# Block-sorted attention and a spatial-gated MLP on one core: a new written order, masks by head pairs, and last output tiles in two goes

## The chip, the core and the metric

The kernel runs on one core of a Trainium2 chip. The core has a matrix engine (TensorE, "PE" in the profile, with its weight loads as "PEld"), a vector engine (VectorE, "DVE"), an engine for activation functions (ScalarE, "ACT"), a general engine (GpSimd, "POOL") and a queue engine (SyncE, "SP"). Sixteen DMA engines move data between the large memory and the core. Matrix products land in PSUM, a memory of eight banks, and another engine has to copy them out. The metric is the device time of one execution in microseconds (us), as the median of several runs. Lower is better.

## What is computed

```python
# q, k, v: 4 batches x 8 heads x 768 positions x 64; sort_net: 4 x 8 x 8 x 8
P = sort_net
for _ in range(5):
    P = np.exp(P - np.max(P, axis=-1, keepdims=True))
    P = P / (np.sum(P, axis=-1, keepdims=True) + 1e-09)
    P = P / (np.sum(P, axis=-2, keepdims=True) + 1e-09)
k_sorted = np.einsum('bhij,bhjcd->bhicd', P, k_b)   # blocks of 96 positions
v_sorted = np.einsum('bhij,bhjcd->bhicd', P, v_b)
attn = softmax(scale * q_b @ k_sorted^T)            # within each block
x = (attn @ v_sorted), heads side by side           # 4 x 768 x 512

h = np.maximum(x @ w_in, 0.0)                       # 512 -> 1024
u, v = h[..., :512], h[..., 512:]
v_n = (v - mean(v)) / np.sqrt(var(v) + 1e-06)
v_s = np.einsum('ts,bsd->btd', w_spatial, v_n) + b_spatial[None, :, None]
out = (u * v_s) @ w_out                             # 4 x 768 x 512
```

## The kernel before

The program is written as small units of work, the functions `u_XX`. One long text, `ORDER` (lines 16 to 49), lists the units in sequence, each with its arguments separated by colons; the loop at the end of the kernel runs through it. Every engine takes its instructions in that order and never overtakes within its own queue. So the order written there sets what stands behind what on each engine, and each DMA queue (loads are issued by POOL, all other transfers by SP) too.

The first argument of a unit that uses TensorE is the PSUM bank at which its tile starts; most tiles take two banks, and the next unit on those banks waits until the last one has been copied out. A letter A, D or P says which engine copies a result out (or does the unit's elementwise part): ACT, DVE or POOL. The following numbers are mostly batch, head pair (of four), and half of the blocks.

- `L` and `LH` load q, k, v (768 KB per batch, cast on the way), the two halves of w_in (`wv`, `wu`), w_spatial (`ws`) and w_out (`wo`), all on POOL's queue (lines 156 to 212). Tiles of q, k and v have two buffers each.
- `SK` is one round of the normalisation of P (lines 243 to 256). `PR` spreads P over partitions with eight small matmuls. `P0` multiplies it by a mask on DVE and so makes the mixing matrix of batch 0 (line 269); `PC` copies it out and `PD` makes the matrices of the other batches on POOL (line 281). `DM` are matmuls on zeros, with no result that is used (line 290).
- `QT` turns q of a head pair (line 324). `KT` mixes and turns k (line 339). For batch 0, `VT` mixes and turns v by the same matmul line, and `VX` turns it back into 96-row blocks (`vb`, line 378). For later batches, `VM` mixes v (`vm`, line 390) and `VC` gathers the blocks by eight DMAs per batch on SP (line 405). `QX` copies q together on DVE or POOL (lines 179 and 181) and turns it by a transposing DMA on SP (line 183), for the third and fourth batches.
- `SC` makes the scores of a head pair and half (line 423) and ACT takes their exponential (line 436). `AT` multiplies by v (line 448). DVE then takes a reciprocal (459) and divides (460). In the form with P, ACT first copies the product out to a scratch tile (`xr`, line 456), and POOL divides. The scratch tile has the tag "z" with two buffers, the same two that `SP` uses for its sums.
- `XT` turns x for batch 0 on TensorE (line 472); `XX` does it by a transposing DMA on SP (line 190) for the others. `WT` is a tiny POOL copy that lets the next load on POOL's queue wait for such a transfer.
- `VP` (line 491) and `UP` (line 536) are the two halves of x @ w_in. `VP` also takes mean and variance on DVE. `LN` and `LA` normalise v, `LA` on DVE or POOL.
- `WS` turns w_spatial by TensorE (line 297). `SP` is the spatial product of 128 columns (line 548), with the bias added on DVE (`z`, line 554) and the product with u (`gt`, line 560) on DVE or POOL. `SH` is half of such a unit (lines 568 to 577).
- `OP` makes two tiles of the output (line 597) and sends them out on SP (line 605). `OH`, used for the last six tiles, makes one (line 583), into one of three buffers (line 587).

In the order before, loads are issued as q (first heads), k, v, q (other heads), `wv`, `wu`, `ws`, then v and k of the second batch, q of the second batch, `wo`, and then the third batch. The fourth batch's loads stand behind a `WT`.

## Time and profile before

| | us |
|---|---|
| median of five runs | 159.28 |
| lowest and highest run | 158.91, 161.5 |
| the profiled execution | 162.13 |
| its span in the trace | 160.2 |

| engine | busy us in the span |
|---|---|
| PE | 143.3 |
| DVE | 117.6 |
| ACT | 83.6 |
| POOL | 53.9 |

| line and work of PE | matmuls | busy us |
|---|---|---|
| 548, spatial product | 180 | 31.2 |
| 536, u half of x @ w_in | 128 | 23.0 |
| 491, v half of x @ w_in | 90 | 22.7 |
| 597, output | 67 | 16.4 |
| 448, attention times v | 256 | 12.7 |

The durations of matmuls overlap, as they are pipelined: twelve of line 548, 0.326 us each, take 1.95 us in the chain of waits. A row's busy time is thus more than it costs the engine, and spacing is read from the chain or the timeline. A few matmul records are missing in a trace. The chain of waits follows the span back from its last instruction, each time to what released it. Its pieces are listed with start, length and what they are. "Issue" in it is time for which the profile shows no cause. The mean granted clock of PE is 0.973 of full speed over the span.

### The profile page before, as it was taken

What the parts mean: (1) busy time and instruction counts of PE and PEld (TensorE: products, weight loads), DVE (VectorE), ACT (ScalarE), POOL (GpSimd) and SP (SyncE); (2) the same over time, 40 slices, a digit from 0 to 9 for tenths busy, and PEclk for the clock granted to TensorE, in tenths of its full rate; (3) what the DMA queues carried; (4) which work ended last, traced back from release to release, by engine and by line L of the source; (5) the groups of instructions that cost most, each with busy time, mean ns of one, the idle gap of its engine ahead of it and who ended that gap; (6) DMA issues with size and microseconds to landing.
All of it is one profiled execution on the core that took longest, in us unless ns stands there. A gap on an engine that the chain in (4) does not pass through costs nothing.

```text
span 160.2 us, 3907 instructions
## 1 busy us (share of the span) xinstructions
PE 143.3 (89%) x1605; PEld 90.5 (56%) x1617; DVE 117.6 (73%) x231; ACT 83.6 (52%) x127; POOL 53.9 (34%) x78
## 2 busy tenths in 40 slices
PE   0399979999998999999799988999999999999780
PEld 0396869755866665565466644655566545555330
DVE  3767867569798589679765999785768878649830
ACT  3325978559969445766754143788743225410140
POOL 7963910474700251060560380061400502500400
PEclk9999996599999999999999999999999999999997
DMA  2999999999999969979999989660745503042073
GB/s 15 198 204 204 207 211 206 203 205 206 226 250 248 192 109 90 227 108 176 220 286 244 194 141 183 109 118 0 262 135 98 97 5 131 0 174 87 0 262 133
DMA packets 36689, 25.49 MB, mean 159 GB/s; under 512 B 16576, under 2 KB 33472, under 8 KB 36672
## 3 DMA queue, kind: packets, MB, share of 16 engines
q0 software_dynamic: 14864, 12.19, 48.9%
q1 hardware_dynamic: 21808, 13.06, 35.6%
q8 instruction: 12, 0.20, 0.5%
q14 instruction: 5, 0.04, 0.1%
HBM read 24.78 MB, written 6.29 MB: 194 GB/s over the span
## 4 chain that ended last, share of the span: by engine, by line
PE 58%; DMA 17%; DVE 12%; issue 5%; SPq 3%; POOL 1%; ACT 1%; DVEq 0%; ACTq 0%; POOLq 0%
PE ps L548 14%; PE ps L536 10%; PE ps L491 10%; DMA vb<-vm 10%; PE ps L597 7%; DMA v_in<-in_v_dram 6%; PE ps L448 4%; PE ps L423 4%; DVE z L554 4%; PE ps L339 3%; SPq L405 3%; DVE gt L560 2%; DVE x_sb L460 1%; DMA out_dram<-oh_sb 1%; DVE stats L505 1%
## 5 line engine op out<-in xcount | busy, mean ns | idle before, releaser
L548 PE MATMUL ps<-wspT,v_sb 128*128 128x384 bf16 x180 | 31.2, 326 | 0.0
L436 ACT ACTIVATE ex<-ps 96x768 bf16<-96x768 f32 x32 | 24.5, 807 | 10.8 <-PE ps L423 10.8
L536 PE MATMUL ps<-xT,w_in_sb 128*128 128x384 bf16 x128 | 23.0, 326 | 0.9 <-DMA xT<-x_sb 0.6
L491 PE MATMUL ps<-w_in_sb,xT 128*128 128x512 bf16 x90 | 22.7, 386 | 0.9 <-DVE z L554 0.4
L548 PEld LDWEIGHTS <-v_sb 128*128 128x128 bf16 x180 | 17.0, 98 | 10.9
L460 POOL TENSOR_TENSOR x_sb<-xr,rec 96x512 bf16<-96x512 f32 x8 | 8.3, 1038 | 40.1 <-DVE rec L459 40.1
L554 DVE TENSOR_TENSOR z<-ps,b_bc 128x768 f32<-128x768 f32 x15 | 14.3, 953 | 5.4 <-PE ps L548 5.3
L505 DVE BATCH_NORM_STATS2 stats<-v_sb 128x6 f32<-128x512 bf16 x24 | 16.3, 678 | 2.5 <-ACT v_sb L114 2.1
L536 PEld LDWEIGHTS <-w_in_sb 128*128 128x128 bf16 x128 | 12.1, 98 | 9.1 <-issue 1.2
L460 DVE TENSOR_TENSOR x_sb<-ps,rec 96x512 bf16<-96x512 f32 x24 | 16.5, 686 | 0.8
L597 PE MATMUL ps<-w_out_sb,gt 128*128 128x512 bf16 x67 | 16.4, 380 | 0.4 <-issue 0.2
L491 PEld LDWEIGHTS <-xT 128*128 128x128 bf16 x96 | 9.2, 100 | 10.7 <-issue 1.2
L522 POOL TENSOR_SCALAR v_sb<-v_sb,nm,rstd 128x512 bf16<-128x512 bf16 x15 | 12.0, 802 | 8.5 <-issue 5.4
L114 ACT ACTIVATE u_sb<-ps 128x768 bf16<-128x768 f32 x12 | 9.7, 810 | 9.4 <-PE ps L536 9.2
L560 DVE TENSOR_TENSOR gt<-z,u_sb 128x768 bf16<-128x768 f32 x12 | 13.6, 1136 | 0.4
L116 DVE TENSOR_SCALAR v_sb<-ps 128x1024 bf16<-128x1024 f32 (+1 forms) x9 | 9.9, 1101 | 5.2 <-PE ps L491 5.1
L448 PE MATMUL ps<-vb,ex 96*128 96x65 bf16 x256 | 12.7, 198 | 1.0 <-DMA vb<-vm 1.0
L448 PEld LDWEIGHTS <-ex 96*128 96x128 bf16 x256 | 10.7, 100 | 3.9 <-issue 1.3
L108 ACT CAST vm<-ps 128x768 bf16<-128x768 f32 x11 | 8.5, 804 | 7.5 <-PE ps L390 7.4
L521 POOL TENSOR_SCALAR nm<-mv 128x1 f32<-128x1 f32 x15 | 3.1, 205 | 25.6 <-DVE mv L506 19.2
L423 PEld LDWEIGHTS <-kT 64*96 64x96 bf16 x256 | 8.0, 122 | 5.0 <-issue 3.6
L108 ACT CAST kT<-ps 128x768 bf16<-128x768 f32 x10 | 8.0, 805 | 5.3 <-PE ps L339 5.3
(91 smaller groups left out, 207.3 us busy)
## 6 DMA issues: line engine op xcount, KB each, us to landing
out_dram<-o_sb SPq DMA_DIRECT2D x9, 512.0 KB, 3.0
k_in<-in_k_dram POOLq DMA_DIRECT2D x4, 768.0 KB, 19.5
v_in<-in_v_dram POOLq DMA_DIRECT2D x4, 768.0 KB, 14.5
vb<-vm SPq DMA_DIRECT2D x24, 99.0 KB, 4.6
q_in<-in_q_dram POOLq DMA_DIRECT2D x3, 768.0 KB, 21.2
out_dram<-oh_sb SPq DMA_DIRECT2D x6, 256.0 KB, 2.1
wsp_nat<-in_moe_w_spatial_dram POOLq DMA_DIRECT2D x1, 1152.0 KB, 19.8
w_in_sb<-in_moe_w_in_dram POOLq DMA_DIRECT2D x2, 512.0 KB, 14.3
```

Of the source, the lines that this page charges most:

```text
L108: nc.scalar.copy(out=out, in_=in_)
L423: nc.tensor.matmul(t[0:BLK, hh, ii * 128:ii * 128 + BLK], lhsT=kT[rows, i * BLK:(i + 1) * BLK], rhs=rhs, start=True, stop=True,)
L436: nc.scalar.activation(out=dst, in_=src, func=AF.Exp, scale=scale)
L448: nc.tensor.matmul(t[:, hh, ii * VW:ii * VW + D + 1], lhsT=e[:, c:c + 128], rhs=vb[b % 2][:, ih * NI + ii, 2 * hp + hh, 0:D + 1], start=Tr ...
L460: (nc.gpsimd if eng == "P" else nc.vector).tensor_mul(out=x_sb[:, hp].rearrange("p i (h d) -> p h i d", h=2), in0=tv[:, :, :, 0:D], in1=_r ...
L491: nc.tensor.matmul(t[:, x, :], lhsT=x_tile(b, n // 3)[:, kc, n % 3 * 128:(n % 3 + 1) * 128], rhs=w_in_sb[:, kc, DH:DFF], start=(kc == 0), ...
L505: nc.vector.bn_stats(out=stats, in_=v_sb[:, x, :])
L536: nc.tensor.matmul(t[:, x, 0:HW], lhsT=w_in_sb[:, kc, mc * 128:(mc + 1) * 128], rhs=x_tile(b, ih)[:, kc], start=(kc == 0), stop=(kc == KC ...
L548: nc.tensor.matmul(t[:, x, 0:HW], lhsT=st["v_sb", b, n][:, mc * 128:(mc + 1) * 128], rhs=wspT[:, n, x * HW:(x + 1) * HW], start=(n == 0), ...
L554: nc.vector.tensor_add(out=z.rearrange("p (x c) -> p x c", x=2), in0=t[:, :, 0:HW], in1=b_bc.rearrange("p (x c) -> p x c", x=2),)
L560: eng.tensor_mul(out=gt, in0=z, in1=st["u", b, mc // 2][:, mc % 2])
L597: nc.tensor.matmul(t[:, x, :], lhsT=st["gt", b, mc][:, c * 128:(c + 1) * 128], rhs=w_out_sb[:, mc, :], start=(mc == 0), stop=(mc == FC - 1),)
```

## The change

The order is written anew throughout: banks, copying engines and the sequence differ in nearly all units. Its parts with a name are these.

The second batch's v and k are loaded ahead of w_spatial, and w_out is loaded behind the third batch's q. The first batch's V is mixed in four whole units (`VT` with a last argument of 2) in place of eight halves. `P0` multiplies the mask for two heads and all blocks at a time, not for four heads and half of the blocks. Five dummies of 384 columns go; twelve of 64 columns are placed between the first `KT`. The memsets of the exponential tiles move from `MK` to `IN`. Thirteen `AT` divide on POOL, eight before. The fourth batch's `QX` is on DVE, before on POOL. `WT` waits for the second batch's x in place of the third batch's q. Ten of the two-tile `VP` are copied by ACT and one by DVE, before four and seven.

The last six output tiles are made in two goes: `OF` issues the matmuls with the first two blocks of columns, `OL` the other two, copies and sends the tile. They have six buffers between them: two of their own, four halves of the `OP` tiles' buffers, and for half of the last tile a "z" tile. The last tile is copied in halves by ACT and DVE and sent by two queues, ACT's and SP's. No `SP` of the fourth batch has its product on POOL, and the two halves of `SH` stand at the two ends of the three last `SP`.

```diff
--- before.py
+++ after.py
@@ -14,38 +14,37 @@
 
 
 ORDER = """
-IN SK:0 LH:q:0:0:4 L:k:0:0:128 ID MK SK:0 L:v:0:0:128 SK:0 QT:0:A:0:1:2 SK:0 QT:2:A:0:0:2 DM:0:12:64
-LH:q:0:4:8 DM:1:12:64 SX L:wv DM:0:12:64 DM:1:12:64 SK:1 DM:0:12:64 DM:1:12:64 PR:0 P0:1:4:8 IV:1
-P0:0:4:8 P0:1:0:4 P0:0:0:4 DM:7:5:384 KT:1:A:0:2:2 PC:A KT:3:A:0:3:2 VT:7:D:1:0 IV:0 VT:5:A:2:0
-KT:1:D:0:1:2 VT:0:A:3:1 KT:6:A:0:0:2 VX:3:D:1:0 SC:1:0:1:0 VX:0:D:3:1 VX:3:D:2:0 QT:4:D:0:2:2
-VT:7:A:0:1 VT:0:D:1:1 VT:1:A:0:0 SC:2:0:1:1 L:wu AT:6:D:0:1:0 L:ws SC:4:0:2:0 L:v:1:0:128 VX:0:D:0:1
-VX:1:D:1:1 L:k:1:0:128 PD:2:4:8 PD:2:0:4 QT:2:A:0:3:2 VT:7:D:2:1 AT:4:D:0:2:0 VX:0:A:0:0 SC:2:0:0:0
...
-SC:2:0:3:1 PD:1:4:8 SC:0:0:2:1 L:q:1:0:128 L:wo AT:6:D:0:3:0 VX:4:D:2:1 XT:2:A:0:1:0 XT:3:D:0:0:0
-XT:7:D:0:0:1 AT:0:P:0:3:1 L:v:2:0:128 AT:4:D:0:2:1 WS:2:A:1 WS:3:A:3 VP:6:D:0:0:1 XT:0:A:0:1:1
-VP:3:D:0:2 VM:4:A:1:1 L:k:2:0:128 VM:6:A:1:0 VP:0:D:0:5 PD:3:0:4 VM:4:A:1:2 VM:1:A:1:3 LN:0:0:3
-VP:6:A:0:3:4 UP:1:A:0:0:0 L:q:2:0:128 KT:6:A:1:2:2 VC:1:0 VC:1:1 KT:4:D:1:3:2 WS:0:D:4 WS:1:A:2
-LN:0:3:6 LA:P:0:2 LA:P:0:1 UP:2:A:0:0:1 WS:7:D:5 QT:4:A:1:1:2 KT:0:D:1:1:2 KT:2:A:1:0:2 LA:D:0:3
...
-WT:q:2:0 L:v:3:0:128 SC:6:2:3:1 SC:2:2:1:0 L:k:3:0:128 OP:4:A:0:2 AT:2:D:2:2:0 L:q:3:0:128 LN:1:0:4
...
-SP:4:D:1:2 AT:6:P:2:1:1 SP:0:D:1:3 XX:2:0 AT:4:P:2:2:1 AT:6:D:2:0:1 SP:2:D:1:1 VM:4:A:3:3 XX:2:1
-QX:P:3 SP:0:D:1:0 VM:4:A:3:2 VM:2:D:3:1 UP:6:A:2:1:0 VP:0:D:2:0:1 VM:6:A:3:0 KT:2:A:3:1:2
-VP:4:A:2:2:3 UP:2:A:2:0:0 KT:4:D:3:0:2 KT:6:A:3:3:2 VC:3:1 LN:2:0:4 KT:0:A:3:2:2 VP:2:D:2:4:5
...
-LA:D:3:4 UP:6:A:3:1:0 LN:3:0:4 LA:D:3:3 LA:P:3:1 LA:P:3:0 UP:4:D:3:0:1 LA:D:3:2 OP:6:A:2:2 OP:4:D:2:0
-SP:6:D:3:2 SP:4:D:3:0 SP:6:P:3:1 SH:4:D:3:3:1 SH:5:D:3:3:0 OH:7:A:3:3 OH:5:D:3:4 OH:4:A:3:0
-OH:7:D:3:5 OH:5:A:3:1 OH:4:A:3:2
+IN LH:q:0:0:4 L:k:0:0:128 ID SK:0 MK SK:0 SK:0 QT:0:A:0:1:2 L:v:0:0:128 IV:1 SX DM:0:12:64
+DM:1:12:64 DM:0:12:64 SK:0 SK:1 DM:1:12:64 QT:2:A:0:0:2 IV:0 LH:q:0:4:8 DM:0:12:64 PR:1 P0:0:2 L:wv
+P0:4:6 P0:6:8 P0:2:4 L:wu L:v:1:0:128 PC:A L:k:1:0:128 L:ws DM:7:9:64 KT:2:D:0:0:2 KT:4:A:0:2:2
+DM:7:2:64 KT:0:D:0:1:2 DM:7:1:64 VT:6:A:1:2 VT:2:D:0:2 SC:4:0:0:1 VT:0:D:2:2 PD:2:0:4 VX:7:D:1:1
+QT:2:A:0:2:2 VX:4:A:0:1 VX:5:D:1:0 SC:0:0:1:1 VX:7:D:2:1 PD:1:0:4 PD:1:4:8 KT:2:D:0:3:2 PD:2:4:8
+VX:4:D:0:0 PD:3:0:4 QT:6:A:0:3:2 VT:0:D:3:2 AT:2:P:0:0:1 L:q:1:0:128 SC:4:0:2:1 VX:7:D:2:0 SC:2:0:3:1
+AT:0:D:0:1:1 SC:6:0:3:0 VX:4:D:3:1 VX:5:A:3:0 AT:2:D:0:2:1 SC:0:0:0:0 AT:6:D:0:3:1 XT:4:D:0:1:0
+AT:2:P:0:3:0 SC:0:0:2:0 XT:7:D:0:1:1 L:v:2:0:128 AT:2:D:0:0:0 SC:4:0:1:0 AT:0:P:0:2:0 UP:6:A:0:0:1
+AT:2:D:0:1:0 VP:0:A:0:5 VM:4:A:1:2 VM:6:D:1:1 XT:2:A:0:0:1 VM:0:D:1:0 XT:3:A:0:0:0 VP:4:A:0:3:4
+VM:2:A:1:3 VP:0:A:0:2 VP:6:A:0:0:1 VC:1:0 LN:0:3:6 UP:2:A:0:1:1 L:k:2:0:128 WS:0:D:5 KT:6:A:1:1:2
+KT:4:A:1:2:2 UP:2:A:0:0:0 LA:D:0:3 KT:6:D:1:0:2 PD:3:4:8 KT:4:A:1:3:2 QT:0:A:1:1:2 WS:2:D:4
+QT:6:D:1:0:2 QT:4:A:1:2:2 QT:2:D:1:3:2 WS:0:D:3 LN:0:0:3 L:q:2:0:128 WS:1:D:0 SC:4:1:2:0 LA:P:0:5
+LA:P:0:4 LA:P:0:1 SC:6:1:0:0 L:wo UP:2:D:0:1:0 VC:1:1 BB AT:0:P:1:2:0 AT:6:D:1:0:0 SC:4:1:1:0 SC:0:1:1:1
...
+UP:0:A:1:1:0 KT:6:D:2:1:2 XX:1:1 KT:4:A:2:3:2 WT:x:1:1 L:v:3:0:128 KT:2:A:2:0:2 OP:0:D:0:0 SC:6:2:1:0
+L:k:3:0:128 SC:2:2:2:0 VP:4:D:1:2:3 SC:2:2:2:1 SC:0:2:0:0 UP:6:A:1:1:1 AT:2:D:2:2:0 AT:4:P:2:1:0
+LN:1:0:4 VP:0:A:1:4:5 UP:4:A:1:0:1 LA:D:1:2 SC:0:2:0:1 LA:P:1:3 SC:2:2:3:0 L:q:3:0:128 OP:6:A:0:2
+LN:1:4:6 AT:0:D:2:0:0 AT:4:D:2:2:1 OP:2:D:0:1 LA:P:1:4 LA:D:1:5 LA:P:1:0 SC:0:2:1:1 SC:4:2:3:1
...
+SC:2:3:1:1 LA:D:2:1 UP:0:A:2:1:0 LA:P:2:0 AT:4:D:3:0:1 AT:6:D:3:3:0 LN:2:4:6 LA:P:2:4 OP:2:D:1:1
...
+SC:2:3:1:1 LA:D:2:1 UP:0:A:2:1:0 LA:P:2:0 AT:4:D:3:0:1 AT:6:D:3:3:0 LN:2:4:6 LA:P:2:4 OP:2:D:1:1
+SC:4:3:1:0 SC:6:3:2:1 LA:D:2:5 OP:0:A:1:2 AT:6:D:3:2:1 AT:2:P:3:3:1 SP:4:D:2:0 AT:2:P:3:1:1
...
+SC:4:3:1:0 SC:6:3:2:1 LA:D:2:5 OP:0:A:1:2 AT:6:D:3:2:1 AT:2:P:3:3:1 SP:4:D:2:0 AT:2:P:3:1:1
+AT:6:P:3:1:0 SP:0:D:2:2 XX:3:1 SC:2:3:2:0 SC:4:3:0:0 OP:6:A:1:0 AT:0:D:3:0:0 AT:4:D:3:2:0 SP:2:P:2:1
+SP:0:D:2:3 UP:2:A:3:1:1 VP:0:A:3:4:5 XX:3:0 UP:2:A:3:0:1 VP:4:A:3:2:3 LN:3:4:6 VP:2:A:3:0:1
+OP:4:A:2:2 LA:P:3:4 LN:3:0:4 LA:P:3:3 LA:D:3:2 LA:D:3:0 LA:P:3:5 LA:P:3:1 UP:2:A:3:0:0 UP:0:A:3:1:0
+OP:4:A:2:0 OP:0:A:2:1 SH:4:D:3:3:0 SP:2:D:3:0 SP:0:D:3:1 SP:2:D:3:2 SH:0:D:3:3:1 OF:1:3:1 OF:2:3:0
+OF:3:3:2 OL:A:3:2 OL:D:3:0 OF:0:3:4 OL:D:3:4 OL:A:3:1 OF:2:3:3 OL:D:3:3 OF:0:3:5 OL:X:3:5
 """
 
 
@@ -215,6 +214,8 @@
         nc.sync.dma_start(out=p_all, in_=sort_net.rearrange("b h i j -> (b h) i j"))
         nc.vector.memset(warm, 0.0)
         nc.vector.memset(eps_tile, 1e-6)
+        for n in range(NE):
+            nc.vector.memset(ex[n][:, 2 * NI * BLK:], 0.0)
 
     def u_BB():
         nc.sync.dma_start(out=b_bc, in_=_raw_ap(moe_b_spatial, 0, [[0, 128], [1, S]]))
@@ -231,8 +232,6 @@
     def u_MK():
         nc.vector.reduce_sum(out=m32, in_=ident.rearrange("p (j t) -> p t j", t=TB), axis=AX.X)
         nc.vector.tensor_copy(out=mask16, in_=m32)
-        for n in range(NE):
-            nc.vector.memset(ex[n][:, 2 * NI * BLK:], 0.0)
 
     def u_IV(n):
         n = int(n)
@@ -262,14 +261,14 @@
                 nc.tensor.matmul(
                     st["pr"][:, ih, ii, :], lhsT=sel[:, ii, :], rhs=p_t[:, ih, :], start=True, stop=True)
 
-    def u_P0(ih, lo, hi):
-        ih, lo, hi = int(ih), int(lo), int(hi)
+    def u_P0(lo, hi):
+        lo, hi = int(lo), int(hi)
         n = hi - lo
-        pr = st["pr"][:, ih]
+        pr = st["pr"]
         nc.vector.tensor_mul(
-            out=pd[0][:, lo:hi, ih * 64:ih * 64 + 64].rearrange("p h (i t) -> p h i t", t=TB),
-            in0=_raw_ap(mask16, 0, [mask16.ap[0], [0, n], [0, NI], [1, TB]]),
-            in1=_raw_ap(pr, lo, [pr.ap[0], [1, n], [BH, NI], [0, TB]]),
+            out=pd[0][:, lo:hi].rearrange("p h (i t) -> p h i t", t=TB),
+            in0=_raw_ap(mask16, 0, [mask16.ap[0], [0, n], [0, NB], [1, TB]]),
+            in1=_raw_ap(pr, lo, [pr.ap[0], [1, n], [BH, NB], [0, TB]]),
         )
 
     def u_PC(eng):
@@ -576,17 +575,48 @@
         eng = nc.vector if gate == "D" else nc.gpsimd
         eng.tensor_mul(out=st["gt", b, mc][:, cols], in0=z, in1=st["u", b, mc // 2][:, mc % 2, cols])
 
+
+    EARLY, LATE = (0, 1), (2, 3)
+
+    def oh_mm(b, c, parts):
+        for mc in parts:
+            nc.tensor.matmul(
+                st["oh", c][:, 0, :], lhsT=st["gt", b, mc][:, c * 128:(c + 1) * 128], rhs=w_out_sb[:, mc, :],
+                start=(mc == EARLY[0]), stop=(mc == LATE[-1]),
+            )
+
+    def u_OF(ps, b, c):
+        st["oh", int(c)] = ps_tile(ps)
+        oh_mm(int(b), int(c), EARLY)
+
+    def oh_tile():
+        n = st["ohn"] = st.get("ohn", -1) + 1
+        if n in (2, 3):
+            return moe.tile([128, DM], FP32, name="oh_sb", tag="oh", bufs=2)
+        if n % 2 == 0:
+            st["oo"] = moe.tile([128, 2, DM], FP32, name="o_sb", tag="o", bufs=2)
+        return st["oo"][:, n % 2]
+
+    def u_OL(eng, b, c):
+        b, c = int(b), int(c)
+        oh_mm(b, c, LATE)
+        t = st["oh", c][:, 0]
+        o_sb = oh_tile()
+        dst = out[b, c * 128:(c + 1) * 128, :]
+        if eng in ("A", "D"):
+            copy(eng, o_sb, t)
+            nc.sync.dma_start(out=dst, in_=o_sb)
+        else:
+            h = DM // 2
+            o2 = moe.tile([128, S], FP32, name="o2", tag="z", bufs=2)[:, 0:h]
+            nc.scalar.copy(out=o_sb[:, 0:h], in_=t[:, 0:h])
+            nc.vector.tensor_copy(out=o2, in_=t[:, h:DM])
+            nc.scalar.dma_start(out=dst[:, 0:h], in_=o_sb[:, 0:h])
+            nc.sync.dma_start(out=dst[:, h:DM], in_=o2)
+
     def u_OH(ps, eng, b, c):
-        b, c = int(b), int(c)
-        t = ps_tile(ps)
-        for mc in range(FC):
-            nc.tensor.matmul(
-                t[:, 0, :], lhsT=st["gt", b, mc][:, c * 128:(c + 1) * 128], rhs=w_out_sb[:, mc, :],
-                start=(mc == 0), stop=(mc == FC - 1),
-            )
-        o_sb = moe.tile([128, DM], FP32, name="oh_sb", tag="oh", bufs=3)
-        copy(eng, o_sb, t[:, 0, :])
-        nc.sync.dma_start(out=out[b, c * 128:(c + 1) * 128, :], in_=o_sb)
+        u_OF(ps, b, c)
+        u_OL(eng, b, c)
 
     def u_OP(ps, eng, b, n):
         b, n = int(b), int(n)
```

## Prediction

> **What bounds the kernel now.** I read the busy shares first, then the granted clock, then the chain of waits, and last the timeline at the three places where the chain leaves TensorE. The page's first part:
>
> ```profile
> span 160.2 us, 3907 instructions
> PE 143.3 (89%) x1605; PEld 90.5 (56%) x1617; DVE 117.6 (73%) x231; ACT 83.6 (52%) x127; POOL 53.9 (34%) x78
> ```
>
> TensorE (PE) is the bound over most of the span: from 32 to 145 us it idles about 3 us in all by the table of windows. A change can therefore win only in the first 30 us, at the few PE idle places, and in the tail. The clock is a term of its own (window row: start:end, length, then busy us of PE, PEld, DVE, ACT, POOL, the clock, DMA share, GB/s):
>
> ```profile
> 26.00:32.00 6.00, 5.78 (x66) 5.17 (x65) 3.33 (x9) 3.78 (x6) 1.88 (x2) 0.50 1.30 203
> 90.00:100.00 10.00, 8.95 (x60) 4.92 (x60) 9.75 (x11) 3.43 (x5) 4.52 (x4) 1.00 1.04 150
> ```
>
> The reader is to see two things: half clock at 26 to 32 us, and a stretch at 90 to 100 us in which VectorE (DVE) is full and PE is not. The chain (start, length, what) names the stalls:
>
> ```profile
> 70.94 8.08 DMA vb<-vm
> ...
> 94.29 2.04 issue
> 96.33 0.96 DVE z L554
> ...
> 152.97 0.59 ACT oh_sb L108
> ...
> 153.58 2.04 DMA out_dram<-oh_sb
> ...
> 155.72 0.59 ACT oh_sb L108
> ```
>
> At 94.29 the chain sits on DVE with nothing that the profile shows as awaited. The timeline there explains it:
>
> ```profile
> 92.70 2.90 POOL L179 TENSOR_SCALAR qx<-q_in 128x1536 bf16<-128x1536 bf16 x2
> 93.31 3.10 DVE L560 TENSOR_TENSOR gt<-z,u_sb 128x768 bf16<-128x768 f32 x1
> ```
>
> A gate product of DVE took 3.10 us while GpSimd (POOL) copied q; the median of the twelve is 0.958.
>
> **The change, part by part.** Nearly every unit moves, so I sum by stage, and look where a named stall goes.
>
> *Work.* The first V is mixed in 4 whole units instead of 8 halves: 48 fewer matmuls. In the chain 36 of that line take 1.12 us, 31 ns each, so PE loses 1.5 us, of early work. Evictions go from ACT 5 x 0.495 + DVE 3 x 0.547 to ACT 0.80 + DVE 3 x 0.95. Five 384-wide dummies (0.99 us) go; they lay beside the mask product, before v landed at 14.05 us: worth 0. P0 by pairs is still four products of 128x256 (4 x 0.42): 0, except that the first K matmul needs one product, not two; v, landing at 14.05, hides that. The small memsets move within idle DVE time: 0. Over the kernel, five attention divisions go from DVE (0.69) to ACT + POOL (0.59 + 1.04), six two-tile relus from DVE (1.22) to ACT (1.02), and the fourth batch's q copy from POOL (2.90) to DVE (2 x 0.96). With the other evictions DVE falls by some 5 us, ACT rises by some 5. ACT stays near 55%.
>
> *Loads.* POOL's queue moved about 205 GB/s without a break to some 53 us. In the old order w_s landed at 27.6 us, second v at 31.6, second k at 35.3, q at 39.2 (issue plus landing). Exchanged: v at about 25.9, k 29.7, w_s 35.5 (1.18 MB at that rate is 5.8 us; v and k take 3.85 each), q 39.3; third v, k, q come 2.6 us earlier, w_out about 53.5. It's an estimate from those rates. POOL's additions in front of a load are few (a 1.04 division before each), and a load is issued several us before its turn.
>
> *First stage, to 37 us.* Walked through unit by unit at full clock with these durations: K 13.1 to 18.7, the last division of batch 0 at 29.2 (before: 30.84, at half clock from 25.4), then the projections (1.71 per pair of tiles, 1.30 per u unit) bring PE to the first w_s transpose at about 37 us, 1.5 us after w_s lands: no wait. Before reached the same amount of PE work near 39.8. How much of those 2.6 us is the half clock I can't separate, since the dip may come again. Bounds: -1.0 (a missed eviction slot) to 2.6. I take **0.5**.
>
> *Clock.* The Trainium skill ("TensorE: Matmul & The Clock Gate", Part 1 and the transpose section) says that the clock halves after an idle window of about 3.4 us and that transposes don't count as busy; by that rule taking warm-up matmuls out speaks against the change. The row: the dip came at 25.4 us, 13 us after the dummies, amid the V and x transposes, and lasted 6.8 us. These transposes stay; the trace shows the half clock but not which operations count as busy. By the row the term is 0; by the rule a second such window would cost up to half of it, 3.4 us. I take 0.
>
> *Second batch's V gather.* Its blocks waited for landing at 49.5 to 51 us (0.17 and 0.25 idle). V comes 5.7 us earlier and its gather is issued by about 36.6 to 39 instead of 43: **0.4** (0 to 0.7).
>
> *Third batch's V gather.* The 8.08 us chain piece ends with PE idle 0.30 and 0.52. Now this gather is issued on SP ahead of the q transpose, some 15 us before its use: **0.8** (0 to 1.2).
>
> *93 to 97 us.* POOL's copy goes to DVE, so the 3.10 us product becomes 0.96; two of the four gate products there go to POOL. DVE gets 1.92 of copies, but behind them stand only K evictions that PE covers with 12 us of other work. PE's idle was 0.62 and 0.38 there: **1.0** (0.3 to 1.5).
>
> The skill's "GPSIMD Engine Reference" (Key points) speaks against the rest of this: POOL shares its SBUF interfaces with DVE when DVE has two SBUF inputs. The two rows agree on the long one (3.10 us), but the change also raises POOL divisions from 8 to 13. By the rule each may hold a gate product up to 1.04 us, 5 x 1.04 = 5.2. By the rows none of the eight old divisions lengthened a gate product (median 0.958), yet none lay fully beside one. Most new ones stand beside matmul evictions, which have one SBUF input at most: I take 0 to 5.2, nearer the row, **-0.5**.
>
> *Tail.* Set zero at 141.38, where PE begins the last spatial product. Before: 7.8 us of spatial products, 1.05 idle behind the POOL gate (1.64), matmuls to 155.5 (14.1), last copy to 156.31 (14.9), because with three buffers the fifth copy waited 1.44 us, and the sixth again, for an earlier tile's output to land. After: half product first (0.97), three whole ones to 6.82, half to 7.8. DVE: z and gate 0.96 each, so the third gate ends at 8.9 and the last half at 10.1. PE runs three early halves of tiles (0.43 each) from 7.8 to 9.1, then a late half needs gate three (8.9), and the last half's gate (10.1) comes before its reader at 10.4. All 24 matmuls stand together: 7.8 + 24 x 0.216 = 13.0. The last tile is copied in halves by ACT and DVE, about 0.4 (prep_sb, 256 wide, took 0.38): 13.5. Landing 2.1 as before. **1.4** (0.7 to 1.8). If the ACT queue's issue is dear, its half alone is late by that.
>
> *Sum.* 0.5 + 0.4 + 0.8 + 1.0 - 0.5 + 1.4 = 3.6. A new order has waits of its own which this reading can't see: the old one kept 3.0 us of PE idle between 32 and 145, of which I took away 1.8 (the 0.4 overlaps the early count); I charge **0.6**. Net 3.0. The profiled execution took 162.13 us, its span 160.2 and 1.9 around it: 162.13 becomes 159.1. That execution is 2.85 above the median of 159.28; the same stalls taken from the median give 156.3.
>
> **Rivals.**
> 1. *Slower: the scratch pair.* A POOL division holds one of the two buffers that the z tiles use too, from ACT's copy until POOL is done. Already before, ACT once waited for it: "xr L456 <- POOL x_sb L460", 2.4 us. The new order puts such divisions three in a row in the fourth batch, and pairs of them among gate products in the second and third. It decides once POOL is over 2 us behind, which is what PE has queued there. At two places 2 x 2.4 = 4.8: 156.3 + 4.8 = 161.1. Against: POOL is only 34% busy. Chance 0.20.
> 2. *Only the tail counts.* The middle's gains come back as other waits: 159.28 - 1.4 = 157.9. For: each stall had other work nearly covering it. Chance 0.20.
> 3. *w_s is late.* PE is 1.5 us behind it by an estimate; if the gathers slow the loads by 3 us, PE stands 1.5: 157.8. Chance 0.08.
> 4. *No dip.* Denser early matmuls keep the clock up: another 2.6, 153.7. Chance 0.07.
>
> **How the numbers follow.** Forecast 0.45, own range 155.2 to 157.5. A measurement can tell about 0.5% (0.8 us) from no change. Faster: 0.45 + 0.07 + 0.06 + most of rival 2 (0.14) = 0.72, less 0.04 for the edges. Same: 0.09. Slower: 0.23, rival 1 and a dip made longer. Range 154.0 to 160.4.
>
> **What would show it.** Right: no DVE gate product near 3 us; no output wait of ACT in the tail, PE ending 13 us after the last stage's first matmul; no V-gather wait in the third batch; w_s landed before its transposes. Wrong: ACT xr or DVE z waiting for POOL for over 2 us at several places, the first w_s transpose waiting for its load, or a clock at half for more than 7 us.

## The result and the profile after

| | us |
|---|---|
| before, median of 39 runs (158.45 to 162.41) | 159.38 |
| after, median of 20 runs (157.46 to 158.87) | 158.19 |
| ratio, with 95% interval | 0.9928 (0.991 to 0.9945) |
| profiled execution after, and its span | 158.62, 156.9 |

By the ratio the change is faster by some 1.15 us, where 3.0 was forecast. The two profiled spans lie 3.3 us apart, not 1.15, because the profiled execution of before went through a stretch at half clock (26 to 32 us) that by their mean clock most of its other runs don't have; the ratio leaves out executions over 1.5% above the fastest. So the later sections use, as a view of the old order, a profile without it, of the old kernel with one edit (e6) or two (e8).

The page after, first part:

```profile
PE 140.0 (89%) x1553; PEld 87.0 (55%) x1564; DVE 109.1 (70%) x225; ACT 87.6 (56%) x132; POOL 56.7 (36%) x81
```

DVE has given up 8.5 us of work and ACT taken 4.0, where some 5 each were counted. PE's share is the same 89%: PE idles no less than before (16.9 us in both spans). The table of windows after shows where (start:end, length, busy us of PE, PEld, DVE, ACT, POOL, clock, DMA share, GB/s):

```profile
40.00:50.00 10.00, 8.88 (x165) 6.78 (x160) 8.40 (x14) 8.43 (x14) 4.42 (x7) 1.00 1.25 243
60.00:70.00 10.00, 9.48 (x100) 4.80 (x101) 6.30 (x9) 5.51 (x7) 0.69 (x2) 1.00 1.00 162
90.00:100.00 10.00, 9.84 (x91) 5.43 (x91) 7.55 (x15) 7.07 (x10) 3.53 (x2) 1.00 0.56 107
100.00:110.00 10.00, 8.27 (x98) 4.86 (x97) 5.51 (x12) 5.91 (x12) 2.81 (x6) 1.00 0.48 83
```

The stall of before at 90 to 100 us is gone (PE 9.84, was 8.95). In its place PE loses 1.7 us ten microseconds later, 0.5 at 60 to 70, and 1.1 at 40 to 50 (PE's busy time there before: 9.90, 9.90 and 9.69). The chain of waits after names the largest (start, length, what):

```profile
98.05 1.03 ACT v_sb L113
...
99.08 0.32 SPq L404
...
103.28 4.15 DMA vb<-vm
```

The chain leaves PE for a copy by ACT, runs through the issue of eight gather transfers on SP one after the other, about 0.6 us each, and returns to PE at 107.47, when the last has landed. What the gather itself stood behind is in the timeline:

```profile
92.52 2.47 DVE L180 COPY qx<-q_in 128x1536 bf16<-128x1536 bf16 x2
92.68 1.89 POOL L559 TENSOR_TENSOR gt<-z,u_sb 128x768 bf16<-128x768 f32 x1 [0.89 <-DVE z L553]
...
95.06 3.68 SPq L182 DMA_TRANSPOSE qX<-qx  x1
...
98.79 5.08 SPq L404 DMA_DIRECT2D vb<-vm  x8
...
107.47 0.31 PE L447 MATMUL ps<-vb,ex 96*128 96x65 bf16 x5 [1.49 <-DMA vb<-vm]
```

The q transpose waits for the q copy, which takes 2.47 us beside POOL's gate product, then keeps SP busy for 3.68 us; the gather, whose data has been ready since 96 us (the last V product's copy by ACT, 95.19 plus 0.80), comes behind it. So the question for the experiments was: are these waits on SP what the forecast's gain went into, or would another wait have taken it anyway?

### The profile page after: what moved, and what is told of

It reads as the page before. It is cut to its first block, busy times and chain, and to the rows that moved or that the text cites. A ratio compares the mean times of both kernels' runs of the same rounds, so it can differ in the third digit from the quotient of the medians.

```text
span 156.9 us, 3816 instructions
## 1 busy us (share of the span) xinstructions
PE 140.0 (89%) x1553; PEld 87.0 (55%) x1564; DVE 109.1 (70%) x225; ACT 87.6 (56%) x132; POOL 56.7 (36%) x81
## 4 chain that ended last, share of the span: by engine, by line
PE 52%; DMA 22%; DVE 12%; issue 4%; SPq 3%; POOL 2%; ACT 2%; DVEq 0%; POOLq 0%; ACTq 0%
DMA v_in<-in_v_dram 13%; PE ps L547 12%; PE ps L627 9%; PE ps L490 8%; PE ps L535 6%; DVE z L553 4%; DVE gt L559 3%; DMA xT<-x_sb 3%; PE ps L583 3%; PE ps L447 3%; DMA q_in<-in_q_dram 3%; PE ps L338 3%; DMA vb<-vm 3%; SPq L404 2%; PE ps L422 2%
## 5 line engine op out<-in xcount | busy, mean ns | idle before, releaser
L459 POOL TENSOR_TENSOR x_sb<-xr,rec 96x512 bf16<-96x512 f32 x13 | 14.1, 1089 | 27.9 <-DVE rec L458 27.9
L490 PE MATMUL ps<-w_in_sb,xT 128*128 128x512 bf16 x91 | 22.1, 380 | 0.8 <-DMA xT<-x_sb 0.4
L113 ACT ACTIVATE v_sb<-ps 128x1024 bf16<-128x1024 f32 (+1 forms) x12 | 11.4, 954 | 9.9 <-PE ps L490 9.9
L113 ACT ACTIVATE u_sb<-ps 128x768 bf16<-128x768 f32 x13 | 10.5, 810 | 6.6 <-PE ps L535 6.2
L447 PE MATMUL ps<-vb,ex 96*128 96x65 bf16 x256 | 12.0, 193 | 2.0 <-DMA vb<-vm 1.7
L107 ACT COPY o_sb<-ps 128x1024 f32<-128x1024 f32 (+1 forms) x7 | 6.7, 951 | 12.3 <-DVE gt L576 8.8
L459 DVE TENSOR_TENSOR x_sb<-ps,rec 96x512 bf16<-96x512 f32 x19 | 13.0, 686 | 0.7
L559 DVE TENSOR_TENSOR gt<-z,u_sb 128x768 bf16<-128x768 f32 x12 | 11.5, 958 | 0.4
L455 ACT COPY xr<-ps 96x520 f32<-96x520 f32 x13 | 7.6, 586 | 7.0 <-POOL x_sb L459 3.7
L627 PEld LDWEIGHTS <-gt 128*128 128x128 bf16 x72 | 6.6, 98 | 7.2
```

Source lines behind the costliest of these rows:

```text
L113: nc.scalar.activation(out=out, in_=in_, func=AF.Relu)
L447: nc.tensor.matmul(t[:, hh, ii * VW:ii * VW + D + 1], lhsT=e[:, c:c + 128], rhs=vb[b % 2][:, ih * NI + ii, 2 * hp + hh, 0:D + 1], start=Tr ...
L459: (nc.gpsimd if eng == "P" else nc.vector).tensor_mul(out=x_sb[:, hp].rearrange("p i (h d) -> p h i d", h=2), in0=tv[:, :, :, 0:D], in1=_r ...
L490: nc.tensor.matmul(t[:, x, :], lhsT=x_tile(b, n // 3)[:, kc, n % 3 * 128:(n % 3 + 1) * 128], rhs=w_in_sb[:, kc, DH:DFF], start=(kc == 0), ...
L559: eng.tensor_mul(out=gt, in0=z, in1=st["u", b, mc // 2][:, mc % 2])
L627: nc.tensor.matmul(t[:, x, :], lhsT=st["gt", b, mc][:, c * 128:(c + 1) * 128], rhs=w_out_sb[:, mc, :], start=(mc == 0), stop=(mc == FC - 1),)
```

## The experiments

In all of them theory A says that the forecast's gains are real and that SP's queue, whose order was changed along with the rest, gives most of them back. The rival B says that PE's waits only trade places.

**The old kernel again (e0), no edit.**

> The kernel before, unchanged, profiled once more. Theory A (the forecast's gains were real, but other waits gave most of them back): without the stretch at half clock the span is 157 to 158 us, and the stalls near 47-51, 76-79, 93-97 us and in the tail are still there, at times some 2 us earlier. Theory B (the first profile's stalls belonged to that one disturbed execution): without the half clock the stalls shrink to less than half of 0.4, 0.8, 1.0 and 1.0 us.

One execution: 161.47 us, span 159.7, with the half clock again. So there was no view without it, and the first part of A's expectation wasn't met. The stalls were all there: PE idle 0.17 and 0.25 near 50 us, 0.31 and 0.60 near 78, 1.42 at 94.4, 0.84 in the tail. As this execution was disturbed too, B doesn't fall with it. It falls with e6 below, whose profile has no half clock and the same stalls (0.26 and 0.25, 0.47 and 0.52, 0.83 in the tail), all but the one that its edit removes.

**The fourth batch's gather ahead of the transpose (e1).**

```diff
-SP:0:P:1:2 QX:D:3 KT:2:A:3:3:2 KT:4:A:3:1:2 VP:6:A:2:0:1 VM:4:A:3:1
+SP:0:P:1:2 VM:4:A:3:1 VC:3:1 QX:D:3 KT:2:A:3:3:2 KT:4:A:3:1:2 VP:6:A:2:0:1
...
-LN:2:0:4 VC:3:1
+LN:2:0:4
```

> The changed kernel with the last of the fourth batch's V products, and half of the gather of its blocks, moved ahead of the transposing DMA of q on SP. Theory A (SP's queue is the chain there: the gather stands behind the 3.7 us issue of the q transpose, and the first products with V wait 1.66 us for it): 1.2 to 1.8 us faster than the changed kernel, so about 156.6 us, ratio to the kernel before 0.983. Theory B (PE's waits only trade places, the next one takes the gain): within 0.4 us of the changed kernel, ratio 0.990 to 0.995.

157.06 us, ratio 0.987 (0.9824 to 0.9916), by the medians 1.1 us below the changed kernel's 158.19, by the ratios 0.9. SP's queue and PE in its timeline:

```profile
92.64 2.61 SPq L405 DMA_DIRECT2D vb<-vm  x4
95.35 4.05 SPq L183 DMA_TRANSPOSE qX<-qx  x1
99.46 2.51 SPq L405 DMA_DIRECT2D vb<-vm  x4
...
105.60 0.65 PE L448 MATMUL ps<-vb,ex 96*128 96x65 bf16 x16
```

The products with V now run as one group of sixteen, with no wait; before they were cut in two by 1.49 us. A holds, with a little less than expected: behind the earlier V product PE waits 0.43 us for ACT's copy near 92 us.

**The third batch's gather behind the x transpose (e2).**

```diff
-AT:2:P:1:2:1 VC:2:1 QX:D:2
+AT:2:P:1:2:1 QX:D:2
...
-XX:1:1 KT:4:A:2:3:2
+XX:1:1 VC:2:1 KT:4:A:2:3:2
```

> The changed kernel with the second half of the third batch's V gather moved behind the q transpose and behind the second x transpose of the second batch on SP. Theory A (the 0.9 us that the v projection waits at 68 us for x is SP's order, x standing behind a gather that nobody needs before 80 us): 0.4 to 0.7 us faster than the changed kernel, ratio 0.989. Theory B: no change, 0.990 to 0.995; the idle returns at the fourth batch's V gather.

157.61 us, ratio 0.991 (0.9878 to 0.9942); by the medians 0.6 us below the changed kernel, by the ratios 0.3, with intervals that overlap. Alone this run doesn't settle it; e4 does. The changed kernel's SP queue, then e2's:

```profile
55.25 3.90 SPq L404 DMA_DIRECT2D vb<-vm  x4
59.24 4.39 SPq L182 DMA_TRANSPOSE qX<-qx  x1
63.73 1.30 SPq L189 DMA_TRANSPOSE xT<-x_sb  x1
```

```profile
56.87 4.25 SPq L183 DMA_TRANSPOSE qX<-qx  x1
61.21 1.46 SPq L190 DMA_TRANSPOSE xT<-x_sb  x1
62.72 3.15 SPq L405 DMA_DIRECT2D vb<-vm  x4
```

In the changed kernel x comes last, issued at 63.73, and PE waits 0.41 us for it from 68.6; in e2 it goes 2.5 us earlier and the v projection doesn't wait.

**The third batch's V products later (e3).**

```diff
-LA:P:0:2 VM:2:D:2:1 LA:P:0:0 VM:4:A:2:0 VM:6:D:2:2 SC:0:1:3:0 WS:2:D:2 SC:4:1:3:1 WS:3:D:1 VM:0:A:2:3 AT:6:D:1:1:0 AT:4:P:1:1:1 VC:2:0 SC:2:1:2:1
+LA:P:0:2 LA:P:0:0 SC:0:1:3:0 WS:2:D:2 SC:4:1:3:1 WS:3:D:1 AT:6:D:1:1:0 VM:0:A:2:3 VM:2:D:2:1 AT:4:P:1:1:1 VM:6:D:2:2 SC:2:1:2:1 VM:4:A:2:0 VC:2:0
```

> The changed kernel with the third batch's V products moved behind two w_s transposes, two score units and one division, some 1.6 us of PE work. Theory A (PE stands 1.2 us at 46 us because v of the third batch lands at 47.0, not at 43.2 as forecast): 0.6 to 1.1 us faster than the changed kernel, ratio 0.987. Theory B: the later gather moves SP's chain on by as much, so the wait for x at 68 us grows by what is won: no change, 0.991 to 0.995.

160.28 us, ratio 1.006 (1.0035 to 1.0085): 2 us slower than the changed kernel, against both theories. The timeline points to the reason:

```profile
45.78 1.50 ACT L436 ACTIVATE ex<-ps 96x768 bf16<-96x768 f32 x2
...
47.34 0.38 PE L423 MATMUL ps<-qT,kT 64*96 64x96 bf16 x8 [1.05 <-ACT ex L436]
```

Without the V products ahead of them, the score units meet PSUM banks that ACT hasn't emptied yet. The V products had filled a hole that ACT leaves anyway. Later PE waits again for copies out of PSUM (0.27, 0.38 and 0.67 us between 50 and 53). In this profile the clock falls to half for some 3.4 us right after, but the dip isn't the loss: three executions of e3 with a mean clock of 1.000 took 160.09 to 160.4 us.

**Both moves on SP (e4), and the changed kernel on the same chip (e5).** Both diffs, of e1 and e2.

> The changed kernel with both moves on SP's queue together: the fourth batch's first half of the V gather ahead of the q transpose, and the third batch's second half behind both transposes. Theory A (two separate waits on SP's queue, 1.1 and 0.6 us each alone): 1.4 to 1.8 us faster than the changed kernel, 156.3 to 156.8 us, ratio 0.981 to 0.984. Theory B (PE's waits trade places): no better than the better of the two, 157.1 us, ratio 0.986 or more.

> The changed kernel itself on the same chip, as the mark for the others: ratio 0.991 to 0.9945 under both theories.

e4: 156.61 us, ratio 0.9859 (0.9832 to 0.9886). e5: 158.3 us, ratio 0.9953 (0.9925 to 0.998), where 0.991 to 0.9945 was expected; the intervals overlap with the first one. Between the two, on one chip, 1.7 us: the gains of e1 and e2 add up (1.1 and 0.6). B falls for these two waits.

**The old kernel with the q copy on DVE (e6).**

```diff
-QX:P:3
+QX:D:3
```

> The kernel before with one letter changed: the fourth batch's q copy on DVE in place of POOL. The forecast's term (the 3.10 us gate product beside POOL's copy becomes 0.96, and PE's idle at 94-97 us of 1.0 to 1.4 us goes): 0.7 to 1.3 us faster, ratio 0.992 to 0.996. Theory A (gained there, given back where the fourth batch's V gather lands some 10 us later): the gate product is short again but PE waits for vb near 108 us, 0 to 0.5 us faster, ratio 0.997 to 1.0.

158.7 us, ratio 0.9963 (0.9925 to 1.0001), about 0.6 us; the interval just reaches no change. This profile is free of the half clock (span 156.5):

```profile
91.79 1.02 DVE L181 COPY qx<-q_in 128x1536 bf16<-128x1536 bf16 x2
...
93.71 0.96 DVE L560 TENSOR_TENSOR gt<-z,u_sb 128x768 bf16<-128x768 f32 x1
```

The gate product is back at 0.96 us, and PE idles nowhere between 77 and 111 us. So A's expectation, that the gain is given back at this batch's V gather, failed on the old order; and yet the gain is only about half of PE's former idle (1.0 us before, 1.42 in e0). Why only half stays open.

**The old kernel with the new tail (e7), and with both (e8).** The new functions for the output in place of `OH`, and in the order:

```diff
-SP:6:D:3:2 SP:4:D:3:0 SP:6:P:3:1 SH:4:D:3:3:1 SH:5:D:3:3:0 OH:7:A:3:3 OH:5:D:3:4 OH:4:A:3:0
-OH:7:D:3:5 OH:5:A:3:1 OH:4:A:3:2
+SH:6:D:3:3:0 SP:2:D:3:0 SP:0:D:3:1 SP:2:D:3:2 SH:0:D:3:3:1 OF:1:3:1 OF:2:3:0 OF:3:3:2 OL:A:3:2
+OL:D:3:0 OF:0:3:4 OL:D:3:4 OL:A:3:1 OF:2:3:3 OL:D:3:3 OF:0:3:5 OL:X:3:5
```

> The kernel before with only the new tail: the order of the last spatial products, no gate product on POOL there, output tiles in two goes and in six buffers. Both theories: PE's end comes 1.0 us earlier in the tail, the rest of the end is about the same; 0.7 to 1.2 us faster, ratio 0.9925 to 0.9955. If the whole gain of the change is the tail, this alone gives the changed kernel's ratio of 0.9928; if other parts add to it, it stays above 0.995.

> The kernel before with just two local edits: the new tail, and the fourth batch's q copy on DVE. Theory A (the new order as a whole, with its loads, masks and whole V, gives nothing beyond these two; its own waits on SP took the rest): 0.9 to 1.3 us faster than before, ratio 0.9915 to 0.9945, as good as the changed kernel. Theory C (the order's other parts are worth the 0.5 to 1.5 us that the forecast counted, and the two edits overlap): ratio 0.996 or more.

e7: 158.75 us, ratio 0.9966 (0.9933 to 0.9998), about 0.5. e8, with the letter of e6 too: 157.94 us, ratio 0.9928 (0.9897 to 0.9959). Two local edits of the old order are worth as much as the whole change. The rest of it, the order of loads, masks, whole V and every other move, comes to nothing in sum. e8's windows show that this isn't because nothing moved:

```profile
70.00:80.00 10.00, 8.88 (x91) 4.95 (x90) 7.66 (x17) 6.14 (x10) 4.70 (x9) 1.00 1.20 222
...
100.00:110.00 10.00, 10.00 (x132) 5.88 (x127) 7.51 (x17) 8.42 (x14) 3.74 (x7) 1.00 0.46 103
```

The old order still has its wait of 1.1 us for the third batch's V at 76 us, which the new one doesn't have; the new one has 1.7 us at 105, which the old one doesn't have.

**The best order with the last tile whole (e9).** e4, and

```diff
-OL:X:3:5
+OL:A:3:5
```

> The changed kernel with both moves on SP's queue and the last output tile copied whole by ACT and sent in one piece. Theory (the two half copies run one after the other, 0.37 and 0.42 us and a gap, against 0.59 for one whole copy, so the split costs 0.2 to 0.3 us): 156.2 to 156.5 us, ratio 0.982 to 0.985. If the split's shorter pieces do land sooner: 156.7 us or more.

156.47 us, ratio 0.9835 (0.9807 to 0.9864), 1.7 us below the changed kernel. Against e4's 156.61 the split is at best worth nothing; 0.14 us is within the two runs' scatter.

**The third batch's v earlier (e10).** The load of the second batch's q is left out, and the first batch's q is used there.

```diff
+        if (x, b) == ("q", 1):
+            st["q", 1] = st["q", 0]
+            return
```

> The changed kernel without the load of the second batch's q (the first batch's q stands in for it), so that the third batch's v lands some 3.9 us earlier. If v's landing at 47 us is a loss of its own: 0.6 to 1.0 us faster than the changed kernel, ratio 0.986 to 0.989. If ACT's exponentials are what paces PE there, as the run with the V products moved behind suggests: within 0.3 us, ratio 0.991 to 0.996.

157.4 us, ratio 0.9899 (0.9857 to 0.9941), some 0.8 us below the changed kernel. Its profile shows no wait for v at 46 us and none for x at 68 us; the 1.6 us at 104.5 stay. So v's landing may cost something after all, where e3 had found no gain in putting it off; but without the 1.6 us behind it this run can't tell how much of a gain survives to the end. e14 repeats it on a better order.

**The changed kernel with the q copy back on POOL (e11).** The letter of e6 the other way.

> The changed kernel with the fourth batch's q copy back on POOL. There it stands behind two gate products of POOL (1.64 us each), so q is copied some 2.9 us after 94.4 us, at about 97.3 and not 95.0, and the q transpose and the V gather on SP move as much. Theory A (SP's chain bounds here): 1.5 to 2.3 us slower than the changed kernel, ratio 1.002 to 1.008. Theory B (the copy only matters where it lengthens a gate product on DVE): no change, 0.991 to 0.996.

159.97 us, ratio 1.0068 (1.0032 to 1.0104), 1.7 to 1.8 us slower than the changed kernel:

```profile
94.13 2.91 POOL L179 TENSOR_SCALAR qx<-q_in 128x1536 bf16<-128x1536 bf16 x2
...
97.07 3.69 SPq L183 DMA_TRANSPOSE qX<-qx  x1
...
102.59 0.56 PE L423 MATMUL ps<-qX,kT 64*96 64x96 bf16 x16 [1.24 <-DMA qX<-qx]
...
108.53 0.56 PE L448 MATMUL ps<-vb,ex 96*128 96x65 bf16 x6 [1.50 <-DMA vb<-vm]
```

The copy ends 2 us later, so does the transpose on SP, and PE now waits for q as well as for V. In this profile there is also a half clock of 3.4 us later on, but it isn't the loss: the executions of e11 with a mean clock of 1.000 took 159.78 to 159.97. In the new order, then, the letter matters because SP's chain hangs on it, not because of a gate product.

**The q copy earlier (e12), and the same on the best order (e13): two misses.** The edit is e12's; e13 has the edits of e9 too, with the fourth batch's last V product behind two K products.

```diff
-SP:6:D:1:1 VM:2:A:3:2
+SP:6:D:1:1 QX:D:3 VM:2:A:3:2
...
-SP:0:P:1:2 QX:D:3 KT
+SP:0:P:1:2 KT
```

> The changed kernel with the fourth batch's q copy one step earlier on DVE, behind the second of the four gate products and ahead of the two that POOL takes. Theory A (the copy's second half takes 2.00 us in place of 0.55 because POOL's gate product runs beside it, and SP's chain starts from it): the copy takes 1.1 us and ends some 4 us earlier, the transpose follows the x transpose on SP near 90 us, PE's wait for vb at 105.9 goes: 1.0 to 1.7 us faster than the changed kernel, ratio 0.983 to 0.988. Theory B (the shared port doesn't matter, the V products or their copies set the gather's time): within 0.4 us of the changed kernel, ratio 0.990 to 0.9955.

> The fastest order so far (both moves on SP, last tile whole), with the q copy early as in e12 and the fourth batch's last V product behind the second K product. Its waits at 92 us of 0.4 to 0.6 us for copies go: 0.1 to 0.6 us below 156.47, ratio 0.980 to 0.983. If PE has nothing more to gain there: 156.3 to 156.7, ratio 0.983 to 0.986.

e12: 162.78 us, ratio 1.0206 (1.0162 to 1.025). e13: 161.42, ratio 1.0095 (1.0056 to 1.0135). Both are slower than the old kernel. e12's timeline:

```profile
88.82 1.02 DVE L181 COPY qx<-q_in 128x1536 bf16<-128x1536 bf16 x2
...
89.91 4.25 SPq L183 DMA_TRANSPOSE qX<-qx  x1
...
94.25 1.48 SPq L190 DMA_TRANSPOSE xT<-x_sb  x1
...
98.39 6.20 PE L491 MATMUL ps<-w_in_sb,xT 128*128 128x512 bf16 x16 [3.98 <-DMA xT<-x_sb]
```

The copy did what it was moved for: 1.02 us, as in e6. But its transpose now stands on SP in front of the third batch's second x transpose, whose data were there, and which gets its turn only at 94.25. PE waits 3.98 us for it. (In e12's profile 6.8 us of half clock follow. They are a part of the loss only: with a mean clock of 0.989 an execution loses at most 1.8 us of 160 by it, and the one of 161.96 us is then still 2 us above the changed kernel.) In e13's profile PE waits 2.36 us for the same x, and 1.26 us for ACT's copy of a K product. This is the mistake of the forecast made a second time: the moved copy was followed on DVE, and the transfer that it starts was not.

**The third batch's v earlier, on the best order (e14).** e9, and the edit of e10: the second batch's q isn't loaded and the first's is used there.

> The fastest order so far (both moves on SP, last tile whole) without the load of the second batch's q (the first batch's stands in). If v's landing at 47 us is a loss of its own, as e10 suggests: 0.3 to 0.8 us below 156.47, ratio 0.979 to 0.982. If e10's gain came from the x wait at 68 us, which this order doesn't have: within 0.2 us, ratio 0.982 to 0.985.

155.88 us, ratio 0.9784 (0.9753 to 0.9814), 0.6 us below e9 (by the ratios 0.8). PE no longer waits for v: it begins the third batch's V products at 46.28 us, in e9's profile at 46.82 and in e17's at 47.07. So v's landing does hold the kernel up, and e3 failed by what it moved into the hole. But e14 takes a load of 768 KB away, so that all later loads come sooner too; that the whole 0.6 is v's isn't shown.

**The x transpose, then the q copy (e15).** As e12, but with the x transpose in front:

```diff
-SP:6:D:1:1 VM:2:A:3:2 SP:4:P:1:0 VM:6:A:3:0 XX:2:1
+SP:6:D:1:1 XX:2:1 QX:D:3 VM:2:A:3:2 SP:4:P:1:0 VM:6:A:3:0
...
-SP:0:P:1:2 QX:D:3 KT
+SP:0:P:1:2 KT
```

> The changed kernel with the third batch's second x transpose issued first (its data are ready near 87.4 us) and the fourth batch's q copy right behind it, both ahead of the last V products. In e12 the q transpose stood in front of that x transpose on SP and PE waited 4 us for x; here it stands behind it. Theory A (the fourth batch's V gather is late only because the q copy beside POOL's gate product and then the q transpose stand in front of it on SP): q copy about 1.0 us near 89, q transpose done by 95 us on SP, gather issued from 96 without a break, no wait of PE for V near 107 us: 1.0 to 1.7 us below the changed kernel, ratio 0.982 to 0.988. B (waits trade places): another wait of over 1 us appears between 90 and 112 us and the time is within 0.5 us of the changed kernel, ratio 0.990 to 0.996. C (the earlier q copy holds back DVE's z tiles near 90 us): PE waits over 0.5 us for a z tile there.

156.48 us, ratio 0.9826 (0.9803 to 0.9849), 1.7 us below the changed kernel. SP's queue:

```profile
84.56 5.22 SPq L190 DMA_TRANSPOSE xT<-x_sb  x2
89.98 4.09 SPq L183 DMA_TRANSPOSE qX<-qx  x1
95.94 5.09 SPq L405 DMA_DIRECT2D vb<-vm  x8
```

The gather begins when its data are there, 2.85 us earlier than in the changed kernel, and PE, busy 9.95 of the ten microseconds from 100, waits for nothing. A holds here, B and C fall: the z tile behind the copy came in time.

**e15 with e9 (e16), and with e2 alone (e17).** e16 adds to e15 the third batch's move of e2 and the whole last tile, and puts the fourth batch's last V product and half of its gather right behind two K products:

```diff
-KT:2:A:3:3:2 KT:4:A:3:1:2 VP:6:A:2:0:1 VM:4:A:3:1
+KT:2:A:3:3:2 KT:4:A:3:1:2 VM:4:A:3:1 VC:3:1 VP:6:A:2:0:1
```

> e9 (both moves on SP, last tile whole), with the x transpose and then the q copy moved as in e15, and the fourth batch's last V product and its gather behind the first two K products instead of ahead of them. A: the 0.6 us that e9's earlier V product cost near 92 us goes, and no wait comes at 107: 0.1 to 0.6 us below e9's 156.47, ratio 0.980 to 0.983. B: another wait takes its place: 156.5 to 157.2, ratio 0.9835 to 0.988.

157.34 us, ratio 0.9879 (0.9858 to 0.99): a miss, 0.9 us above e15.

```profile
91.52 1.50 ACT L108 CAST kT<-ps 128x768 bf16<-128x768 f32 x2 [1.23 <-PE ps L339]
...
93.07 0.48 PE L390 MATMUL ps<-v_in,pd 128*128 128x384 bf16 x2 [1.26 <-ACT kT L108]
```

The V product goes into the PSUM banks (4 in the order's letters) that the K product just ahead of it still holds, and PE waits for their copy. e17 leaves that product where the changed kernel has it; it is e15 with e2's move and the whole last tile.

> e15 with the third batch's gather moved as in e2 and the last tile whole as in e9; the fourth batch's last V product stays where the changed kernel has it. In e16 it stood right behind a K product of the same PSUM banks, and PE waited 1.26 us for that product's copy (ACT kT at 91.52, 1.50 long); here that wait has no cause. A (the waits on SP are separate and add up): no wait for x at 68 us, none for V at 105 to 108, none over 0.3 us at 91 to 93: 0.4 to 0.8 us below e15's 156.48, ratio 0.9765 to 0.980, the fastest of all. B (waits trade places): 156.2 to 157.2, ratio 0.981 to 0.988.

155.86 us, ratio 0.9755 (0.9735 to 0.9775): by the medians 2.3 us below the changed kernel (by the ratios 2.8), and the fastest that computes all of the reference. No wait for x or for the mixed V is left; PE's largest idle is 0.73 us at 46.3, for the load of v. The windows of e17:

```profile
60.00:70.00 10.00, 9.90 (x115) 5.41 (x116) 6.75 (x10) 5.68 (x8) 2.01 (x3) 1.00 1.01 176
...
100.00:110.00 10.00, 9.95 (x120) 5.89 (x120) 6.36 (x14) 7.41 (x13) 2.83 (x6) 1.00 0.27 65
```

## Why the forecast was wrong in size

The direction was right, and so was the sum's frame: PE's work in the tail came out as walked, from 138.97 in the chain to 151.96, the 13.0 us of the forecast. All four of its signs of being right came true as well: no gate product on DVE over 0.96 us, no output wait of ACT in the tail and these 13 us, no gather wait in the third batch, and w_spatial landed at 35.37, before its first transpose at 36.66. They tested the terms that were counted as gains, and none tested the waits that the new order brings. Term by term:

| term | forecast us | what the runs show |
|---|---|---|
| first stage | 0.5 | not tried alone |
| second batch's gather | 0.4 | wait gone (e6: 0.26 and 0.25), not tried alone |
| third batch's gather | 0.8 | wait gone (e6: 0.47 and 0.52), not tried alone |
| 93 to 97 us | 1.0 | 0.6 (e6), on the old order |
| divisions on POOL beside gate products | -0.5 | 0: no gate product on DVE over 0.96 |
| tail | 1.4 | 0.5 (e7) |
| other waits | -0.6 | -2.3 behind SP's queue (e17), up to -0.6 at v's landing (e14) |

The last column doesn't add up to the 1.15 measured: with the forecast's own figures for the three terms not tried alone it gives -0.1. Some 1.2 us of the gain are not traced to a term; each run removes its term in another surrounding. That e17 stands 3.5 us below the old kernel (3.9 by the ratio), about the 3.6 counted before the charge, is thus in part luck: the tail and the stretch at 93 us gave 1.3 less than counted.

*The step that failed is the charge for other waits.* "I charge 0.6" was set from the old order's leftover idle. The waits behind SP's queue alone take more: two moves on SP give 1.7 back (e4 against e5), and e17, which also moves the q copy that starts SP's transfers and leaves the last tile whole (some 0.1 by e9), gives back 2.3. They could have been read in the order beforehand: the forecast said of the q copy that behind it "stand only K evictions that PE covers with 12 us of other work". It followed the copy on DVE and not on SP, where the q transpose (3.7 us of issue) and then eight gather transfers (0.6 us each) stand behind it, and the products with V behind them. From the changed kernel's rows: 92.5, plus 2.5 for the copy, 3.7 for the transpose, 4.5 to the start of the eighth transfer and 4.15 for its landing, is 107.4, where PE went on at 107.47. The old profile had the transpose (3.7), the transfers (4.5) and a landing of 3.8 for this gather. The same goes for the second batch's x: the gather that was moved up "on SP ahead of the q transpose" was counted as a gain, and what it was moved in front of wasn't.

*The shared port* was weighed at the wrong instruction. The forecast set 0.5 aside for gate products beside POOL's divisions; all twelve took 0.96 at most. But the q copy that the change brings to DVE has halves of 0.55 us undisturbed (e6), and in the profile after, one half took 2.00 us beside POOL's gate product, which took 1.89 instead of 1.64:

```profile
L180 DVE COPY qx<-q_in x4: 507/548/2003, 55.8 to 93.0; 128x1536 bf16<-128x1536 bf16 x4
```

(This row of the tile's instructions gives minimum, median and maximum in ns, and the first and last start.) The forecast priced the copy at 2 x 0.96 from the old profile, where one of the two halves was 1.38. The long half ended at 95.0, some 0.4 us behind the end of POOL's product (94.57), as if it had waited for the whole of it. So the rule of the Trainium skill's "GPSIMD Engine Reference" (Key points) did bite, for 1.45 us: not by its second clause, two SBUF inputs, which the forecast used, but with a copy of one input, for which the page names a 2-port mode of DVE (no row shows the mode). And it bit at the head of SP's chain, where the wait behind it was 1.49. e15 ends both at once: its copy takes 0.55 and 0.51. A run in which only the copy gets faster, at its old place, wasn't made.

*Loads.* The third batch's k and q landed 2.6 us earlier, as forecast (50.8 and 54.6, before 53.4 and 57.2), v only 1.4 (46.98, before 48.34), and w_out, put at 53.5, at 58.35. The forecast's rate of 205 GB/s (3.9 us for 768 KB) left out for v what it had weighed for w_spatial alone (rival 3): the second batch's V gather runs at the same time, and the one load beside it takes almost twice as long. In the changed kernel v landed 7.5 us behind the load before it, in the old one 6.6; in e10, where v goes ahead of the gather, it landed 3.8 us behind the load before it, and k behind it took 7.4. By that rate the gather's eight transfers of 99 KB are 3.9 us, an estimate that fits the 3.6 more. So PE, which reaches that place sooner in the new order, waits:

```profile
47.02 1.15 PE L389 MATMUL ps<-v_in,pd 128*128 128x384 bf16 x6 [0.85 <-DMA v_in<-in_v_dram]
```

In e5, the same kernel again, PE comes 0.5 us later, doesn't wait and goes on at 46.75; the span is no longer for it (156.5 against 156.9). So what PE gains earlier is lost here. The w_spatial load was on time: rival 3 didn't occur.

*Tail.* PE's idle did go; by the timeline it was 0.83 us (before and e6), not the 1.05 of the chain. The other 0.4 was a misreading: ACT's wait of 1.44 us for an output was real, but the last matmul ended at 155.52 and the last copy began at 155.72, so by then the wait cost 0.2 us at most. And behind the last matmul the new tail is 0.2 us longer: 4.8 us to the end of the span in e8, 4.6 in e6, as two half copies stand where one stood and the last output took 2.6 us to land, not 2.4. PE's end 0.8 us earlier less 0.2 is what e7 and e8 show. The split of the last tile bought nothing:

```profile
152.03 0.37 ACT L612 COPY o_sb<-ps 128x256 f32<-128x256 f32 x1 [1.19 <-PE ps L583]
...
152.43 0.42 DVE L613 COPY o<-ps 128x256 f32<-128x256 f32 x1 [0.62 <-ACT o_sb L612]
```

DVE's half waits for ACT's: both read one PSUM bank, and the program makes them take turns. The Trainium skill, "PSUM — Partial Sum Buffer" (Terms, the entry on the PSUM bank), says that two engines reading one bank at once collide, which would be a reason for the turn-taking; no run here tries it without. 0.37 and 0.42 in sequence are longer than one copy of 0.59.

*Rivals.* Rival 2 came nearest: 157.9, where 158.19 was measured, "the middle's gains come back as other waits". That is what happened. It had the tail at 1.4 where 0.5 came, and its reason, that each stall had other work nearly covering it, isn't what the runs show: on the old order the gain at 93 us stays (e6), and it is the new order's own queue that takes as much away. The scratch pair (rival 1): ACT waited for POOL 3.7 us in all, twice, up to 2.2, but PE behind it only 0.17. The half clock (rival 4) did become rarer, and the ratio hardly counts it: a mean clock under 0.985 stands in 9 of the old kernel's 33 executions beside e5, in none of e5's 13 and none of the 20 above. Its term of 0, for taking warm-up matmuls out, held. What decides a dip was not tried; e3 and e12, close to the changed kernel, have it again (3 of 22 and 3 of 6).
